# Attention projections in five token blocks of 384, 384, 384, 416 and 480 tokens instead of five blocks of 384 and one of 128

## The chip, the cores and the metric

One core of one Trainium2 chip. The metric is the device time of one execution in microseconds (us). "Before" took 1542.9 us, the median of 3 runs (1540.59 to 1543.96). Profiles come from one execution each.

## The reference, cut to what matters

The result is `x + A(xn) + B(xn)` with `xn` the normalized input of 2048 tokens by 1024. `B` is a mixer with an MLP; the change doesn't touch it. `A` is attention over 64 segments of 32 tokens with 8 memory rows that pass from one segment to the next:

```python
for s in range(n_seg):                       # 64 segments of 32 tokens
    h = jnp.concatenate([mem, xs], axis=1)   # 8 memory rows + 32 tokens
    q, k, v = (jnp.einsum('btd,dhe->bhte', h, W) for W in (Wq, Wk, Wv))   # 32 heads of 128
    p = _softmax(jnp.where(mask, q @ k.T * scale, -1e9))
    o = jnp.einsum('bhte,hed->btd', p @ v, Wo)
    mem = o[:, :M, :]
    outs.append(o[:, M:, :])
```

The kernel computes all segments in parallel. It keeps one speculated memory row for each later segment (the first has 8), so there are 2048 + 71 = 2119 columns to project. A check at the end decides whether a serial path is needed; it isn't in these runs.

## The kernel before: the parts that matter

A "tile" is three segments: 96 tokens and 3 memory rows, 99 columns (the first 106; the last, with one segment, 33). A block is four tiles: about 396 columns. The last 128 tokens form a sixth block of one full and one 33-column tile, run together with the fifth block as one group. For each block and each group of four heads (eight "head groups") the kernel projects queries and keys, computes scores, normalizes, transposes the probabilities by a DMA, and multiplies them with the values.

```python
groups = ((0,), (1,), (2,), (3,), (4, 5))
LAT = 10.0
# ... for each group, each head group hg:
for w, dsts, scale in ((wq, QTs, QSCALE), (wk, KTs, None)):
    for hh in range(4):
        for B, dst in zip(Bs, dsts):
            proj(B, w, hh, dst, scale)                       # 8 matmuls
            tick(8 * (B["nb"] / 2400 + 0.0025), ...)         # see below
        # ... output projection of the block before, in pieces, each with a tick
```

```python
def proj(B, w, hh, dst, scale):
    nb = B["nb"]
    ps = psum.tile([P, 512], F32, tag="mm", bufs=4)
    for k in range(KT):     # KT = 8; blocks 0 and 5 read one run of columns, the others four pieces of 99 (step 104)
        nc.tensor.matmul(ps[:, :nb] ..., w[:, k, hh * P:(hh + 1) * P], B["rhs"](k), start=(k == 0), stop=(k == KT - 1))
    # ... copied to dst by ScalarE
```

`tick` is a schedule made at build time. It advances an estimated clock, issues at most one pending load item (half a weight matrix, or all the values of a block), and emits at most one score item and one output item that are due. Outputs are due `LAT` = 10 us after their scores:

```python
def tick(us, blocked=None):
    clock[0] += us
    turn[0] += 1
    if turn[0] % every == 0:      # every = 1
        load_some(1)
    # ... emit one due score item ("S") and one due output item ("O")
```

The values of the 128-token block are four small transfers, which make one load item:

```python
nc.sync.dma_start(V[0:96, 0, :], V_d[r:r + 96, cs_])
nc.sync.dma_start(V[0:32, 1, :], V_d[r + 96:r + 128, cs_])
nc.sync.dma_start(V[96:99, 0, :], Vr_d[67:70, cs_])
nc.sync.dma_start(V[32:33, 1, :], Vr_d[70:71, cs_])
```

The transposes of the probabilities stand in the same SyncE queue:

```python
nc.vector.tensor_tensor(Pn[:T, :, :T], e[:T, :, :T], rs[:T, :].unsqueeze(2).to_broadcast((T, 4, T)), op=ALU.mult)
# ...
nc.sync.dma_start_transpose(PTr, Pn[:rows].rearrange("p h k -> p (h k)"))
```

## Time and profile before

| | before |
|---|---|
| time, first runs | 1542.9 us (3), with two more 1541.85 us (5) |
| span of the profiled execution | 1545.1 us |
| TensorE busy | 98% |
| fourth block, from its first projection to the fifth's | 140.2 us |
| last group (blocks 4 and 5), from its first projection to the closing matmuls of the memory rows | 211.6 us |

From the head of the page of before, with busy us, share of the span and number of instructions of each engine:

```profile
span 1545.1 us, 25390 instructions
PE 1514.8 (98%) x10308; PEld 839.7 (54%) x10382; DVE 523.8 (34%) x1092; ACT 513.9 (33%) x1218; POOL 192.5 (12%) x272
PEclk9999999999999999999999999999999999999999
```

TensorE sets the time: it is never idle for long, at full granted clock but for its two ends and one stretch of 3.4 us at half clock near 598 us, before the attention. What one matmul costs can't be read from the groups. These lines are from the groups by shape of before (busy us, mean ns of one):

```profile
L639 PE MATMUL ps<-hTb,wt 128*128 128x396 bf16 x2048 | 387.6, 332 | 0.0
L639 PEld LDWEIGHTS <-wt 128*128 128x128 bf16 x3072 | 264.5, 97 | 148.1 <-DMA wt<-in_A_Wq_dram 2.1
...
L639 PE MATMUL ps<-hTb,wt 128*128 128x132 bf16 x512 | 40.0, 221 | 0.0
```

A mean of 221 ns for 132 columns suggests that small matmuls are wasteful. They aren't: matmuls overlap. The cost is the distance from one start to the next. These lines are from TensorE's timeline of before (start us, length us; consecutive instructions merged):

```profile
1308.39 0.35 PE L678 MATMUL psO<-PT,V 99*128 99x99 bf16 x4 [1.15 <-DMA PT<-Pn]
1308.58 1.52 PE L639 MATMUL ps<-hTb,wt 128*128 128x396 bf16 x8
1309.93 0.35 PE L654 MATMUL psS<-KT,QT 128*99 128x99 bf16 x4
1310.12 0.62 PE L639 MATMUL ps<-hTb,wt 128*128 128x132 bf16 x8
1310.58 0.34 PE L678 MATMUL psO<-PT,V 99*128 99x99 bf16 x4
```

Eight matmuls of 396 columns take 1309.93 - 1308.58 = 1.35 us, 169 ns each; eight of 132 take 0.46 us, 57.5 ns each. Over all neighbours in the trace the means are 169.4 and 57.6 ns. "Start-to-start" below is this distance.

The first line also shows the one real wait of the attention: output matmuls that wait for the transposed probabilities. The line of TensorE's waits in the last group of before (us in total, times, longest):

```profile
PE psO L678 <- DMA PT<-Pn: 3.8, 5, 1.6
```

The profile counts idle time there, 3.8 us; the start-to-start excess over a plain matmul at these places is 4.6 us, because a matmul's modelled end overlaps the wait. SyncE's queue shows why in part. The longest of these waits ends at 1435.06 us. Below are the output in TensorE's timeline, SyncE's timeline ahead of it, and two lines of SyncE's waits in the last group:

```profile
1435.06 0.35 PE L678 MATMUL psO<-PT,V 99*128 99x99 bf16 x4 [1.57 <-DMA PT<-Pn]
```

```profile
1425.68 0.50 SPq L724 DMA_DIRECT2D wt<-in_A_Wk_dram  x1
1426.28 1.24 SPq L669 DMA_TRANSPOSE PT<-Pn  x1
1427.61 0.56 SPq L623 DMA_DIRECT2D V<-V_scratch  x1
1428.22 0.37 SPq L628 DMA_DIRECT2D V<-Vmem_scratch  x1
1428.75 0.32 SPq L630 DMA_DIRECT2D V<-V_scratch  x1
1429.12 0.46 SPq L631 DMA_DIRECT2D V<-V_scratch  x1
1429.63 0.59 SPq L632 DMA_DIRECT2D V<-Vmem_scratch  x1
1430.27 0.31 SPq L633 DMA_DIRECT2D V<-Vmem_scratch  x1
1432.45 7.32 SPq L669 DMA_TRANSPOSE PT<-Pn  x4
```

So the five waits of this profile have two origins. By start-to-start excess, two (0.75 and 0.45 us) follow a transpose issued 3.7 and 3.6 us late behind a weight load; two (1.7 and 0.4 us) follow one issued at most 0.9 us late that took 8.7 and 7.0 us to land; one (1.3 us) has both, 2.2 us late and 6.5 us to land.

The stretches of the third and fourth block and the last group in before (stretch, its us, then busy us of each engine, clock, DMA share, GB/s):

```profile
1011.10:1150.90 139.80, 139.59 (x961) 80.98 (x962) 64.70 (x136) 63.61 (x160) 9.99 (x16) 1.00 0.77 191
1150.90:1291.10 140.20, 139.86 (x961) 80.81 (x962) 64.53 (x138) 63.12 (x160) 11.73 (x18) 1.00 0.82 197
1291.10:1502.70 211.60, 207.20 (x1769) 129.11 (x1776) 98.62 (x225) 96.29 (x293) 8.11 (x16) 1.00 0.56 131
```

Only the last group has time in which TensorE (the first busy number) isn't busy: 4.4 us.

### The profile page before, as it was taken

The numbers are of one execution on the slowest core, as the hardware profiler recorded it, in microseconds if no ns is written. First come the engines' busy times: TensorE is split into PE (matmuls) and PEld (weight loads), VectorE is DVE, ScalarE is ACT, GpSimd is POOL, SyncE is SP. The second block draws the span as 40 slices with busy tenths as digits, with TensorE's granted clock in tenths as the row PEclk, the third lists the DMA queues.
The fourth block names the chain that finished last, engine by engine and source line by source line (L and its number), as shares of the span: only waits on it lengthen the run. The fifth ranks groups of instructions, "written<-read, shape, count | busy, mean of one in ns | idle before, by whom it ended". The sixth has DMA issues, their size and how long they took to land. (4 is left out here: it accounts for less than half of the span.)

```text
span 1545.1 us, 25390 instructions
## 1 busy us (share of the span) xinstructions
PE 1514.8 (98%) x10308; PEld 839.7 (54%) x10382; DVE 523.8 (34%) x1092; ACT 513.9 (33%) x1218; POOL 192.5 (12%) x272
## 2 busy tenths in 40 slices
PE   7999999999999999999999999999999999999998
PEld 7844444444444444444456645654665566466654
DVE  8284010000200111111246624651663365235541
ACT  5533202103012011111156614651662366056620
POOL 5232020221211241010000011002000200100001
PEclk9999999999999999999999999999999999999999
DMA  7679543452353998542389947992997599458611
GB/s 251 182 213 311 205 148 125 143 184 83 130 164 87 215 275 273 173 124 83 123 231 252 235 129 179 246 237 73 239 239 175 129 249 227 111 130 198 136 45 50
DMA packets 288601, 270.39 MB, mean 175 GB/s; under 512 B 137459, under 2 KB 255368, under 8 KB 288480
## 3 DMA queue, kind: packets, MB, share of 16 engines
q1 hardware_dynamic: 265088, 185.53, 47.0%
q0 software_dynamic: 23392, 83.19, 16.8%
q8 instruction: 83, 1.36, 0.4%
q14 instruction: 38, 0.31, 0.1%
HBM read 190.73 MB, written 46.73 MB: 154 GB/s over the span
## 5 line engine op out<-in xcount | busy, mean ns | idle before, releaser
L639 PE MATMUL ps<-hTb,wt 128*128 128x396 bf16 (+2 forms) x3072 | 514.9, 314 | 1.3 <-DMA wt<-in_A_Wq_dram 1.3
L639 PEld LDWEIGHTS <-wt 128*128 128x128 bf16 x3072 | 264.5, 97 | 148.1 <-DMA wt<-in_A_Wq_dram 2.1
L569 PE MATMUL ps<-wt,xT 128*128 128x512 bf16 x1004 | 222.0, 381 | 4.1 <-ACT Vs L571 3.1
L697 PE MATMUL pso<-wo_sb,oX 128*128 128x512 bf16 x1000 | 223.2, 379 | 1.4 <-issue 0.2
L515 PE MATMUL ps<-xn3T,w_sb 128*128 128x512 bf16 x896 | 195.9, 379 | 1.1 <-ACT h3T L516 1.1
L540 PE MATMUL ps<-w_sb,h3T 128*128 128x512 bf16 x872 | 194.3, 379 | 1.2
L569 PEld LDWEIGHTS <-xT 128*128 128x128 bf16 x1024 | 100.6, 98 | 125.3 <-issue 5.6
L516 ACT ACTIVATE h3T<-ps 128x512 bf16<-128x512 f32 x112 | 66.5, 597 | 292.0 <-PE ps L515 289.0
L697 PEld LDWEIGHTS <-oX 128*128 128x128 bf16 x1024 | 98.9, 98 | 115.3
L645 ACT CAST KT<-ps 128x396 bf16<-128x396 f32 (+1 forms) x192 | 87.1, 456 | 189.6 <-PE ps L639 186.5
L515 PEld LDWEIGHTS <-w_sb 128*128 128x128 bf16 x896 | 86.8, 98 | 103.9 <-issue 1.3
L540 PEld LDWEIGHTS <-h3T 128*128 128x128 bf16 x896 | 86.8, 98 | 102.8
L660 DVE TENSOR_REDUCE sums<-sm 99x4 f32<-99x396 f32 (+1 forms) x176 | 97.6, 555 | 113.9 <-ACT sm L658 113.9
L647 ACT ACTIVATE QT<-ps 128x396 bf16<-128x396 f32 (+1 forms) x192 | 89.4, 469 | 108.0 <-PE ps L639 79.8
L656 DVE TENSOR_TENSOR sm<-psS,c_mask_reg_sb 99x396 f32<-99x396 f32 x160 | 91.4, 572 | 90.1 <-PE psS L654 89.9
L571 ACT CAST Vs<-ps 128x512 bf16<-128x512 f32 x64 | 37.2, 586 | 238.4 <-PE ps L569 152.6
L658 ACT ACTIVATE sm<-sm 99x396 f32<-99x396 f32 (+1 forms) x176 | 92.7, 527 | 65.9 <-DVE sm L656 64.7
L573 DVE CAST Vs<-ps 128x512 bf16<-128x512 f32 x64 | 44.2, 692 | 181.8 <-PE ps L569 156.8
L666 DVE TENSOR_TENSOR Pn<-sm,rs 99x396 bf16<-99x396 f32 (+1 forms) x176 | 99.0, 562 | 10.2 <-DMA PT<-Pn 4.0
L541 DVE TENSOR_TENSOR R<-ps,R 128x512 f32<-128x512 f32 x32 | 22.1, 692 | 231.4 <-PE ps L540 215.0
L704 POOL DMA_DIRECT2D out_dram<-ot x32 | 17.5, 546 | 575.8 <-DVE ot L703 569.9
L679 ACT CAST oX<-psO 128x384 bf16<-128x384 f32 x176 | 82.5, 469 | 16.8 <-PE psO L678 16.7
(116 smaller groups left out, 979.5 us busy)
## 6 DMA issues: line engine op xcount, KB each, us to landing
wt<-in_A_Wq_dram SPq DMA_DIRECT2D x78, 512.0 KB
wt<-in_A_Wk_dram SPq DMA_DIRECT2D x78, 512.0 KB
wt<-in_A_Wv_dram POOLq DMA_DIRECT2D x24, 1024.0 KB, 7.1
V_scratch<-Vs SPq DMA_DIRECT2D x32, 512.0 KB
V<-V_scratch SPq DMA_DIRECT2D x40, 384.0 KB
w_sb<-in_B_w_dram SPq DMA_DIRECT2D x9, 1024.0 KB
R_scratch<-x POOLq DMA_DIRECT2D x16, 512.0 KB, 4.4
R<-R_scratch SPq DMA_DIRECT2D x16, 512.0 KB
```

The costliest lines, as they stand in the source:

```text
L515: nc.tensor.matmul(ps[:].rearrange("p (n t) -> p n t", t=P), w3_sb[:, k, f * P:(f + 1) * P], xn3T[tb][:, :, k, :], start=(k == 0), stop=(k ...
L540: nc.tensor.matmul(ps[:], h3T[:, f, j * P:(j + 1) * P], w4_sb[:, f, ch * 512:(ch + 1) * 512], start=(f == 0), stop=(f == FT - 1))
L569: nc.tensor.matmul(ps[:], xT[:, m4 * 4 + j, k, :], wv[:, k, :], start=(k == 0), stop=(k == KT - 1))
L639: nc.tensor.matmul(ps[:, :nb] if B["b"] in (0, 5) else ps[:, :nb].rearrange("p (t c) -> p t c", t=4), w[:, k, hh * P:(hh + 1) * P], B["rhs ...
L645: nc.scalar.copy(o, i)
L647: nc.scalar.mul(o, i, scale)
L656: nc.vector.tensor_tensor(sm[:T, :, :T], S3, t["mask"][:].unsqueeze(1).to_broadcast((T, 4, T)), op=ALU.add)
L658: nc.scalar.activation(e[:T, :, :T], sm[:T, :, :T], ACTF.Exp, scale=LN2)
L660: nc.vector.tensor_reduce(ss, e[:T, :, :T], axis=AX.X, op=ALU.add)
L666: nc.vector.tensor_tensor(Pn[:T, :, :T], e[:T, :, :T], rs[:T, :].unsqueeze(2).to_broadcast((T, 4, T)), op=ALU.mult)
L679: nc.scalar.copy(oX[:, hs_, t["tok"]:t["tok"] + nt], O3[:, :, 0:nt])
L697: nc.tensor.matmul(self.ps[:], self.oX[:, h, self.gl * P:(self.gl + 1) * P], wo_sb[:, h, self.cc], start=(h == 0), stop=(h == H - 1))
```

## The change

The intent: no extra 128-token block. Its 33-column tile joins the fourth block (4 x 99 + 33 = 429 columns) and its full tile the fifth (5 x 99 = 495 columns, within the 512 of the tile `ps` that a projection writes). The 512 matmuls of 132 columns, their weight loads and 64 evacuations (ScalarE's copies of the results) go. The core of the diff; address arithmetic, buffers and names are cut:

```diff
-        if b == 5:
-            segs = (3, 1)
-        else:
-            segs = (3, 3, 3, 3)
+        gis = list(range(4 * b, 4 * b + 4)) + ([21] if b == 3 else [20] if b == 4 else [])
@@ block_setup
+            elif b == 3:
+                hTb = early.tile([P, KT, 432], BF16, tag="hTb")
+                for t in tl:
+                    nc.gpsimd.dma_start(hTb[:, :, t["c0"]:t["c0"] + t["ntok"]], xT_d[...])
+                    d = t["c0"] + t["ntok"]
+                    nc.vector.tensor_copy(hTb[:, :, d:d + t["nm"]], MZ[:, :, t["r0"]:t["r0"] + t["nm"]])
             else:
-                hTb = early.tile([P, KT, 4, 104], BF16, tag="hTb")
+                hTb = early.tile([P, KT, nt, 104], BF16, tag="hTb")     # nt = 5 in the last block
@@ load_values: the four loads of block 5 go; block 3 has two small loads more
+            if b == 3:
+                nc.sync.dma_start(V[0:32, 4, :], V_d[S - 32:S, cs_])
+                nc.sync.dma_start(V[32:33, 4, :], Vr_d[70:71, cs_])
@@
-        groups = ((0,), (1,), (2,), (3,), (4, 5))
+        groups = ((0,), (1,), (2,), (3,), (4,))
```

The attention output of the 33-column tile is kept in the last 32 columns of block 3's output buffer, which block 4 goes on to use. The small sums `xsum` move from the constants to a buffer that is freed earlier.

More of the change, by code (lines that the diff above doesn't have):

```diff
@@ L141 @@
     nc.vector.memset(neghalf[:], -0.5)
-    xsum = cpool.tile([P, KT, NSEG], BF16)
     sums = cpool.tile([P, NTILE * 8, 4], F32)
@@ L158, in tiles_of @@
     def tiles_of(b):
-        if b == 5:
-            segs = (3, 1)
-        else:
-            segs = (3, 3, 3, 3)
-        out_, c, t0 = [], 0, 4 * b
-        for i, s in enumerate(segs):
+        gis = list(range(4 * b, 4 * b + 4)) + ([21] if b == 3 else [20] if b == 4 else [])
+        out_, c = [], 0
+        for i, gi in enumerate(gis):
+            s = 1 if gi == 21 else 3
             first = b == 0 and i == 0
@@ L167, in tiles_of @@
             msk = mask_first if first else (mask_reg if s == 3 else mask_last)
-            r0 = 0 if first else 7 + 3 * (t0 + i)
-            out_.append(dict(c0=c, ntok=s * SEG, nm=nm, T=s * SEG + nm, mask=msk, r0=r0, tok=i * 96, i=i, gi=t0 + i))
+            r0 = 0 if first else 7 + 3 * gi
+            out_.append(dict(c0=c, ntok=s * SEG, nm=nm, T=s * SEG + nm, mask=msk, r0=r0, tok=i * 96, i=i, gi=gi))
             c += s * SEG + nm
@@ L195 @@
             w3ctx = bctx.enter_context(ExitStack())
+            xctx = bctx.enter_context(ExitStack())
+            xsum = xctx.enter_context(tc.tile_pool(name="xs", bufs=1)).tile([P, KT, NSEG], BF16)
             w3_pool = w3ctx.enter_context(tc.tile_pool(name="w3", bufs=1, side="right"))
@@ L549 @@
                         nc.gpsimd.dma_start(R_v[:, n, :], R1[:])
+            xctx.close()
             vsp = vctx.enter_context(tc.tile_pool(name="vsp", bufs=3, side="right"))
@@ L600, in block_setup @@
                 hTb, rhs = hTb0, lambda k: hTb0[:, k, :nb]
-            elif b == 5:
-                hTb = early.tile([P, KT, 136], BF16, tag="hT5", bufs=1)
-                nc.gpsimd.dma_start(hTb[:, :, 0:96], xT_d[:, :, a:a + 96])
-                nc.gpsimd.dma_start(hTb[:, :, 99:131], xT_d[:, :, a + 96:a + 128])
-                nc.vector.tensor_copy(hTb[:, :, 96:99], MZ[:, :, 67:70])
-                nc.vector.tensor_copy(hTb[:, :, 131:132], MZ[:, :, 70:71])
+            elif b == 3:
+                hTb = early.tile([P, KT, 432], BF16, tag="hTb")
+                for t in tl:
+                    nc.gpsimd.dma_start(hTb[:, :, t["c0"]:t["c0"] + t["ntok"]], xT_d[:, :, 96 * t["gi"]:96 * t["gi"] + t["ntok"]])
+                    d = t["c0"] + t["ntok"]
+                    nc.vector.tensor_copy(hTb[:, :, d:d + t["nm"]], MZ[:, :, t["r0"]:t["r0"] + t["nm"]])
                 rhs = lambda k: hTb[:, k, :nb]
             else:
-                hTb = early.tile([P, KT, 4, 104], BF16, tag="hTb")
+                nt = len(tl)
+                hTb = early.tile([P, KT, nt, 104], BF16, tag="hTb")
                 r0 = tl[0]["r0"]
-                for i in range(4):
+                for i in range(nt):
                     nc.gpsimd.dma_start(hTb[:, :, i, 0:96], xT_d[:, :, a + 96 * i:a + 96 * (i + 1)])
-                nc.vector.tensor_copy(hTb[:, :, :, 96:99], MZ[:, :, r0:r0 + 12].rearrange("p k (t r) -> p k t r", t=4))
+                nc.vector.tensor_copy(hTb[:, :, :, 96:99], MZ[:, :, r0:r0 + 3 * nt].rearrange("p k (t r) -> p k t r", t=nt))
                 rhs = lambda k: hTb[:, k, :, 0:99]
@@ L616, in block_setup @@
                     t["c0"] = 104 * i
-            return dict(b=b, tiles=tl, nb=nb, ntok=ntok, rhs=rhs, cols=nb if b in (0, 5) else 416)
+            return dict(b=b, tiles=tl, nb=nb, ntok=ntok, rhs=rhs, cols=nb if b in (0, 3) else 104 * len(tl))
         def load_values(B, V, hg):
             b, cs_ = B["b"], slice(hg * 512, (hg + 1) * 512)
-            r = 384 * b
-            if b < 5:
-                nc.sync.dma_start(V[0:96, 0:4, :], V_d[r:r + 384, cs_].rearrange("(t p) c -> p t c", p=96))
-                if b == 0:
-                    nc.sync.dma_start(V[96:106, 0, :], Vr_d[0:10, cs_])
-                    nc.sync.dma_start(V[96:99, 1:4, :], Vr_d[10:19, cs_].rearrange("(t j) c -> j t c", j=3))
-                else:
-                    nc.sync.dma_start(V[96:99, 0:4, :], Vr_d[7 + 12 * b:19 + 12 * b, cs_].rearrange("(t j) c -> j t c", j=3))
-            else:
-                nc.sync.dma_start(V[0:96, 0, :], V_d[r:r + 96, cs_])
-                nc.sync.dma_start(V[0:32, 1, :], V_d[r + 96:r + 128, cs_])
-                nc.sync.dma_start(V[96:99, 0, :], Vr_d[67:70, cs_])
-                nc.sync.dma_start(V[32:33, 1, :], Vr_d[70:71, cs_])
+            r, n = 384 * b, 5 if b == 4 else 4
@@ new lines, in load_values @@
+            nc.sync.dma_start(V[0:96, 0:n, :], V_d[r:r + 96 * n, cs_].rearrange("(t p) c -> p t c", p=96))
+            if b == 0:
+                nc.sync.dma_start(V[96:106, 0, :], Vr_d[0:10, cs_])
+                nc.sync.dma_start(V[96:99, 1:4, :], Vr_d[10:19, cs_].rearrange("(t j) c -> j t c", j=3))
+            else:
+                nc.sync.dma_start(V[96:99, 0:n, :], Vr_d[7 + 12 * b:7 + 12 * b + 3 * n, cs_].rearrange("(t j) c -> j t c", j=3))
+            if b == 3:
+                nc.sync.dma_start(V[0:32, 4, :], V_d[S - 32:S, cs_])
+                nc.sync.dma_start(V[32:33, 4, :], Vr_d[70:71, cs_])
@@ L635, in proj @@
         def proj(B, w, hh, dst, scale):
-            nb = B["nb"]
+            nb, nt = B["nb"], len(B["tiles"])
+            flat = B["b"] in (0, 3)
             ps = psum.tile([P, 512], F32, tag="mm", bufs=4)
             for k in range(KT):
-                nc.tensor.matmul(ps[:, :nb] if B["b"] in (0, 5) else ps[:, :nb].rearrange("p (t c) -> p t c", t=4), w[:, k, hh * P:(hh + 1) * P], B["rhs"](k), start=(k == 0), stop=(k == KT - 1))
-            if B["b"] in (0, 5):
+                nc.tensor.matmul(ps[:, :nb] if flat else ps[:, :nb].rearrange("p (t c) -> p t c", t=nt), w[:, k, hh * P:(hh + 1) * P], B["rhs"](k), start=(k == 0), stop=(k == KT - 1))
@@ L641, in proj @@
+            if flat:
                 o, i = dst[:, hh, :nb], ps[:, :nb]
             else:
-                o, i = dst[:, hh, :].rearrange("p (t c) -> p t c", t=4)[:, :, 0:99], ps[:, :nb].rearrange("p (t c) -> p t c", t=4)
+                o, i = dst[:, hh, :].rearrange("p (t c) -> p t c", t=nt)[:, :, 0:99], ps[:, :nb].rearrange("p (t c) -> p t c", t=nt)
             if scale is None:
@@ L670, in scores, with outputs @@
             return PTr
-        def outputs(t, hg, PTr, V, oX):
+        def outputs(t, hg, PTr, V, oX, at):
             T, nt = t["T"], t["ntok"]
@@ L678, in outputs @@
                 nc.tensor.matmul(O3[:, hh, :], V[:T, t["i"], hh * P:(hh + 1) * P], PTr[:T, hh, :T], start=True, stop=True)
-            nc.scalar.copy(oX[:, hs_, t["tok"]:t["tok"] + nt], O3[:, :, 0:nt])
+            nc.scalar.copy(oX[:, hs_, at:at + nt], O3[:, :, 0:nt])
             nq = t["nm"]
@@ L720, in stage_loads @@
             wq, wk = ready or (wtile(), wtile())
-            Vs = [qkv.tile([P, len(B["tiles"]), 512], BF16, tag=f"V{B['b'] // 5}", bufs=3, name=f"V{B['b']}") for B in Bs]
+            Vs = [qkv.tile([P, len(B["tiles"]), 512], BF16, tag="V", bufs=3, name=f"V{B['b']}") for B in Bs]
             for w, src in () if ready else ((wq, Wq_v), (wk, Wk_v)):
@@ L757 @@
                 wq, wk, Vs = ahead
-                QTs = [qkv.tile([P, 4, B["cols"]], BF16, tag=f"QT{B['b'] // 5}", name=f"QT{B['b']}") for B in Bs]
-                KTs = [qkv.tile([P, 4, B["cols"]], BF16, tag=f"KT{B['b'] // 5}", name=f"KT{B['b']}") for B in Bs]
+                QTs = [qkv.tile([P, 4, B["cols"]], BF16, tag="QT", name=f"QT{B['b']}") for B in Bs]
+                KTs = [qkv.tile([P, 4, B["cols"]], BF16, tag="KT", name=f"KT{B['b']}") for B in Bs]
                 if hg == 2 and gi_ + 1 < len(groups):
@@ L782, with s_item @@
                     if B["b"] not in oXs:
-                        if B["b"] == 5:
-                            oXs[5] = early.tile([P, H, B["ntok"]], BF16, tag="hTb", name="oX5")
-                        else:
-                            oXs[B["b"]] = abig.tile([P, H, B["ntok"]], BF16, tag="oX", name=f"oX{B['b']}")
-                    def s_item(t=t, hg=hg, QT=QT, KTt=KTt, V=V, oX=oXs[B["b"]], due=due, gi_=gi_):
+                        oXs[B["b"]] = oX_last if B["b"] == 4 else abig.tile([P, H, 512 if B["b"] == 3 else 384], BF16, tag="oX", name=f"oX{B['b']}")
+                        oX_last = oXs[B["b"]]
+                    oX, at = oXs[B["b"]], 480 if t["gi"] == 21 else t["tok"]
+                    def s_item(t=t, hg=hg, QT=QT, KTt=KTt, V=V, oX=oX, at=at, due=due, gi_=gi_):
                         PTr = scores(t, hg, QT, KTt)
                         def o_item():
-                            outputs(t, hg, PTr, V, oX)
+                            outputs(t, hg, PTr, V, oX, at)
                             return 0.18
@@ L796 @@
                     smalls.append((due, ("S", gi_), s_item))
-            outs = [Out(oXs[B["b"]], 3 * B["b"] + gl, gl, ch) for B in Bs for gl in range(B["ntok"] // P) for ch in range(2)]
+            outs = [Out(oXs[B["b"]], 3 * B["b"] + gl, gl, ch) for B in Bs for gl in range(4 if B["b"] == 4 else 3) for ch in range(2)]
         head, rest = outs[:4], outs[4:]
```

## The prediction

> **What bounds it.** TensorE: the page gives 1514.8 busy of 1545.1 us (98%) at full granted clock. A group's mean duration is no cost here, because matmuls overlap; I take start-to-start distances from the timeline: 512 columns 215.7 ns, 403 columns 171, 396 columns in four pieces of 99 169.4, 132 columns 57.6. The Trainium skill ("TensorE: Matmul & The Clock Gate", section "Wait — 56ns, not 53.3ns?") states N / 2.4 GHz + about 2.5 ns warm; the flat shapes agree (132: 55.0 + 2.6; 512: 213.3 + 2.4), the shape in four pieces pays 4.4. Weight loads (97 ns in the groups) are hidden even behind 57.6 ns matmuls, so a small block is not a wasteful matmul.
>
> **What the change removes, adds and moves.** The last group's projections drop from 512 matmuls of 396 plus 512 of 132 columns to 512 of 495 (five pieces); the fourth block's 512 go from 396 to 429 (flat). Columns are the same (2119 per weight tile); 512 matmuls and weight loads go. Score, output and closing matmuls keep their counts (22 tiles of 8 head groups); the 33-row tile moves to the fourth block. ScalarE loses 64 evacuations (about 0.28 us each, 18 us), but at 33% busy that is off the path. Estimate: before 169.4 + 169.4 + 57.6 = 396.4 ns per set, after about 181.4 + 210.6 = 392; 512 times 4.4 ns is 2.3 us, all on the path.
>
> **Waits.** In the last group (about 1310 to 1490 us) the output matmuls wait for the transposed probabilities (the DMA PT<-Pn): start-to-start excesses of 1.7, 1.3, 0.75, 0.45 and 0.4 us, 4.6 us in all, while the middle blocks lose about 0.3 each. From scores to output the schedule gives about 10.4 us; the median transposition lands in 7, but in the last group the time from probabilities to the transpose's issue on SyncE's queue rises to 2.0 us (upper quartile) against under 0.1 in the middle blocks: that queue also carries six loads of values per head group there (four small ones for the 128-token block) besides four of weights and six transposes. After, the last block has two value loads and five transposes, the fourth four and five. I expect the last block to lose under 1 us, the fourth 1 to 1.5: some 2 us saved net, less certain than the matmul term.
>
> The output projection, the tail and the first 1160 us: unchanged.
>
> **Predicted: 1538.6 us** (1542.9 - 2.3 - 2.0), range 1535 to 1542.5. Faster by over 2%: 1%; within 2%: 98.5%; slower by over 2%: 0.5%.
>
> **What would show it.** Right: 512 matmuls each of 429 and 495 columns, start-to-start 181-182 and 209-212 ns; ScalarE about 15 us less busy; the fourth block's window grows by about 10 us, the last's falls by about 14; PT waits of the last block below 1 us, of the fourth 1 to 1.5. Wrong: 495 columns costing over 215 ns; PT<-Pn waits of 4 us or more still there, moved to the fourth block; a new wait for ScalarE or for V loads, since five tiles now meet eight projections.
>
> **What would make it wrong.** The wait term: transposes come in the fourth block as densely as in the old last group (13 queue entries per about 13.4 us against 16 per 16.6), so the gain may be 2.3 us alone (about 1540.6), or the waits may grow. The runs of before differ among themselves by 3.4 us, more than half of what I predict.

## More of the kernel before

```profile
SPq L669 <- DMA wt<-in_A_Wk_dram: 11.2, 6, 2.9
...
SPq L633 <- DMA wt<-in_A_Wk_dram: 2.1, 2, 1.1
```

The transpose that this output waited for is the one at 1426.28, between a weight load and six value loads. It was issued 0.44 us after its probabilities were done and landed at 1435.02, 8.7 us after its issue (median of the last group's tiles: 2.7): it was late on its way, not in the queue. The next transpose, at 1432.45, was late in the queue: it was issued 3.1 us after its probabilities, and landed in time for its output all the same. The trace shows what held it. SyncE's DMAs signal their landing on eight semaphores in turn, and before each issue SyncE waits for the semaphore that it will use. The eighth entry before this transpose is the weight load at 1425.68; that load landed at 1432.39, and the transpose was issued 0.06 us later. The line of 11.2 us counts six such waits, one in each of six head groups.

## The result, and the profile after

After took 1540.13 us, the median of 5 runs (1538.93 to 1540.65), against 1541.85 us of before (5 runs). The ratio is 0.9981, with a 95% interval of 0.9966 to 0.9996. Ratios here are the mean time of one kernel's runs over that of the other's runs of the same rounds, so they are not quite the ratio of the medians. In a later batch after took 1540.01 us against 1544.77 us: 0.9966 (0.9953 to 0.9979). So the gain is 3 to 5 us: 2.9 us by the first ratio (interval 0.6 to 5.2) and 5.2 us by the second (3.2 to 7.3). Both are far within 2%.

From the head of the page of after:

```profile
span 1538.9 us, 24379 instructions
PE 1516.0 (99%) x9870; PEld 810.3 (53%) x9870; DVE 522.2 (34%) x1094; ACT 506.1 (33%) x1154; POOL 192.5 (13%) x272
```

The busy us of TensorE are no measure of the gain. They rose by 1.2 us while the span fell by 6.2 us, and its instruction count fell by 438 where the program has 512 matmuls less, so 74 more records were missing from the trace of before. The new shapes among the groups of after:

```profile
L638 PEld LDWEIGHTS <-wt 128*128 128x128 bf16 x2560 | 233.9, 97 | 168.3 <-DMA wt<-in_A_Wq_dram 1.8 <-issue 0.7
L638 PE MATMUL ps<-hTb,wt 128*128 128x396 bf16 x1024 | 193.6, 332 | 0.0
L638 PE MATMUL ps<-hTb,wt 128*128 128x495 bf16 x512 | 117.3, 373 | 0.0
L638 PE MATMUL ps<-hTb,wt 128*128 128x429 bf16 x512 | 102.7, 345 | 0.0
```

TensorE's timeline of after, once in the fourth and once in the last block:

```profile
1270.96 1.62 PE L638 MATMUL ps<-hTb,wt 128*128 128x429 bf16 x8
1272.41 0.34 PE L677 MATMUL psO<-PT,V 99*128 99x99 bf16 x4
...
1401.15 1.85 PE L638 MATMUL ps<-hTb,wt 128*128 128x495 bf16 x8
1402.84 0.35 PE L653 MATMUL psS<-KT,QT 128*99 128x99 bf16 x4
```

Start-to-start: 1.45 us for 8, 181 ns; 1.69 us for 8, 211 ns. The means over the trace are 181.9 and 211.1 ns.

The same three stretches in after:

```profile
1011.00:1151.60 140.60, 140.01 (x965) 81.09 (x963) 64.54 (x140) 62.81 (x161) 10.87 (x17) 1.00 0.74 190
1151.60:1301.80 150.20, 150.20 (x1016) 82.11 (x1014) 70.72 (x162) 68.64 (x181) 10.86 (x17) 1.00 0.73 187
1301.80:1496.40 194.60, 194.60 (x1211) 98.55 (x1210) 91.06 (x198) 83.84 (x209) 8.07 (x16) 1.00 0.54 138
```

In the fourth and last blocks TensorE is busy all the time; the list of its waits there is empty. In the third block, whose program did not change except that it prepares the next block's input, a wait of TensorE has come in, and on VectorE its origin:

```profile
PE psS L653 <- ACT KT L644: 0.6, 1, 0.6
```

```profile
1081.09 0.19 DVE L606 COPY hTb<-MZ 128x24 bf16<-128x24 bf16 x1 [1.37 <-DMA hTb<-xT_scratch]
...
1084.88 0.18 DVE L606 COPY hTb<-MZ 128x24 bf16<-128x24 bf16 x1 [2.32 <-DMA hTb<-xT_scratch]
1084.97 0.56 DVE L655 TENSOR_TENSOR sm<-psS,c_mask_reg_sb 99x396 f32<-99x396 f32 x1
```

In the new layout of the fourth block's input the copies of memory rows lie between the loaded columns, and each waits for the load written before it. The next tile's scores start on VectorE right after the last copy, at 1084.97, having stood behind its wait of 2.3 us; the delay then passes to ScalarE and to TensorE (a_mz_first below tests this).

The lengths of the stretches, by the start of the first projection matmul of each block and of the closing memory matmuls, are the sharpest measure, since they hold no launch or start-up:

| us | third block | fourth | last | fourth + last |
|---|---|---|---|---|
| before, first profile | 139.8 | 140.2 | 211.6 | 351.7 |
| before, second profile | 139.8 | 139.8 | 210.0 | 349.8 |
| after, first | 140.5 | 150.2 | 194.6 | 344.8 |
| after, second | 140.4 | 150.2 | 194.6 | 344.8 |

After gives the same length twice; before does not.

### The profile page after: what moved, and what is told of

The parts are those of the page before. It is cut to its first block, busy times and chain, and to the rows that moved or that the text cites. A ratio compares the mean times of both kernels' runs of the same rounds, so it can differ in the third digit from the quotient of the medians. Undisturbed runs are those within 1.5% of the kernel's fastest.

```text
span 1538.9 us, 24379 instructions
## 1 busy us (share of the span) xinstructions
PE 1516.0 (99%) x9870; PEld 810.3 (53%) x9870; DVE 522.2 (34%) x1094; ACT 506.1 (33%) x1154; POOL 192.5 (13%) x272
## 5 line engine op out<-in xcount | busy, mean ns | idle before, releaser
L638 PE MATMUL ps<-hTb,wt 128*128 128x396 bf16 (+3 forms) x2560 | 509.9, 343 | 1.0 <-DMA wt<-in_A_Wq_dram 1.0
L638 PEld LDWEIGHTS <-wt 128*128 128x128 bf16 x2560 | 233.9, 97 | 168.3 <-DMA wt<-in_A_Wq_dram 1.8
L644 ACT CAST KT<-ps 128x396 bf16<-128x396 f32 (+3 forms) x160 | 82.0, 513 | 221.8 <-PE ps L638 219.9
L659 DVE TENSOR_REDUCE sums<-sm 99x4 f32<-99x396 f32 (+2 forms) x176 | 97.5, 554 | 113.2 <-ACT sm L657 113.2
L657 ACT ACTIVATE sm<-sm 99x396 f32<-99x396 f32 (+2 forms) x176 | 92.7, 527 | 76.3 <-DVE sm L655 75.7
L646 ACT ACTIVATE QT<-ps 128x396 bf16<-128x396 f32 (+3 forms) x160 | 83.8, 525 | 74.9 <-PE ps L638 50.2
L665 DVE TENSOR_TENSOR Pn<-sm,rs 99x396 bf16<-99x396 f32 (+2 forms) x176 | 98.9, 562 | 6.2 <-DMA PT<-Pn 0.2
L678 ACT CAST oX<-psO 128x384 bf16<-128x384 f32 (+1 forms) x176 | 82.5, 469 | 9.0 <-PE psO L677 8.5
```

The source lines that it names most:

```text
L638: nc.tensor.matmul(ps[:, :nb] if flat else ps[:, :nb].rearrange("p (t c) -> p t c", t=nt), w[:, k, hh * P:(hh + 1) * P], B["rhs"](k), star ...
L644: nc.scalar.copy(o, i)
L646: nc.scalar.mul(o, i, scale)
L657: nc.scalar.activation(e[:T, :, :T], sm[:T, :, :T], ACTF.Exp, scale=LN2)
L659: nc.vector.tensor_reduce(ss, e[:T, :, :T], axis=AX.X, op=ALU.add)
L678: nc.scalar.copy(oX[:, hs_, at:at + nt], O3[:, :, 0:nt])
```

## The experiments

Theory M: TensorE pays for columns plus a small fixed amount for each matmul, and weight loads are hidden. Theory Q: the waits of the last group come of the many entries of SyncE's queue, or of their coming in a burst; from its experiments came theory B (the burst alone). Rival S: they come of too short a distance from scores to outputs. Rival W: small matmuls are bounded by their weight loads. Three times below are worked out from the trace's records, as medians or quartiles over the tiles of a block: "issue delay" is the time from the end of the probabilities' last operation to the start of the transpose on SyncE's queue, "to landing" is from the last score matmul to the transpose's last semaphore update, and "waits" are start-to-start excesses of over 0.2 us at output matmuls that wait for it.

| run | fourth + last, us | ratio to before | 95% |
|---|---|---|---|
| c_before_again | 349.8 | 0.9992 | 0.9978 to 1.0005 |
| b_v5_pool | 352.6 | 1.0016 | 0.9999 to 1.0033 |
| b_later_out | 347.5 | 0.9977 | 0.9960 to 0.9995 |
| b_paced | 346.6 | 0.9988 | 0.9974 to 1.0003 |
| a_burst | 352.0 | 1.0020 | 1.0006 to 1.0034 |
| a_split | 346.2 | 0.9982 | 0.9968 to 0.9996 |
| a_mz_first | 344.8 | 0.9976 | 0.9962 to 0.9990 |
| a_flat | 344.0 | 0.9950 | 0.9935 to 0.9966 |
| after_again | 344.8 | 0.9966 | 0.9953 to 0.9979 |
| a_halves | 347.5 | 1.0001 | 0.9987 to 1.0014 |
| a_flat_late | 344.0 | 0.9951 | 0.9927 to 0.9974 |

The first four shared a chip, so did the next four, and the last three. The medians of before were 1544.57, 1543.42 and 1544.77 us there. A ratio's interval is about 2 us wide to each side, so the stretches tell more than the ratios where the question is 1 us.

### c_before_again: before against itself

No edit.

> The kernel before, unchanged, timed against itself. It tells the noise of a ratio and whether the first profile of before (span 1545.1 us, 4.6 us of start-to-start excess at output matmuls of the last group that wait for PT<-Pn) is a typical execution. Theory Q (the waits are a fixed property of the program): ratio 1.000 within 0.15%, and the new profile shows again 3.5 to 5.5 us of such excess. Rival R (the first profile caught an unlucky execution): the new profile shows under 2.5 us of excess and a span of 1540 to 1543 us.

Measured: 1543.23 us, ratio 0.9992; span of the profiled execution 1540.2 us. TensorE's waits in the last group:

```profile
PE psO L678 <- DMA PT<-Pn: 2.4, 2, 1.6
```

The start-to-start excess was 2.9 us, between what the two theories expected. The wait is a property of the program, but its size varies from execution to execution, and the first profile of before (span 1545.1 us) had caught a larger one. So the 6.2 us between the two profiled spans overstate the gain.

### b_v5_pool: the small value loads moved to another queue

```diff
-                nc.sync.dma_start(V[0:96, 0, :], V_d[r:r + 96, cs_])
+                nc.gpsimd.dma_start(V[0:96, 0, :], V_d[r:r + 96, cs_])
# and so for the other three
```

> Before, with the four small value loads of the 128-token block issued from GpSimd instead of SyncE; nothing else. Theory Q (the transposes are issued late because they stand behind these loads in SyncE's queue): time from probabilities to issue of the transposes in the last group falls from 2.0 us (upper quartile) to under 0.5, the PT waits of the last group from 4.6 us to under 1.5, and the time by 1 to 4 us. Rival S (the wait comes of the short distance from scores to outputs, 10.3 us in this group, with a transpose that simply takes long): issue delay may fall, but waits stay over 3 us and the time stays within 0.5 us.

Measured: 1548.06 us, ratio 1.0016. The issue delay vanished (upper quartile 0.08 us, from 2.0), exactly as theory Q expected, and the waits did not, as rival S expected:

```profile
PE psO L678 <- DMA PT<-Pn: 4.0, 6, 1.0
```

The transposes were issued earlier and took longer: from issue to landing 6.7 us at the upper quartile, against 4.0 in before. To landing stayed at 9.7 us (before: 9.8). So standing behind these four loads in the queue is not what makes the transposes late; take the queue away, and they are late elsewhere. The Trainium skill ("DMA: Bandwidth & Descriptors", section "Issuing engines are not separate DMA queues") says that DMAs issued from different engines run on the same 16 DMA engines, and that issuing from several saves only the issue time; this run fits that: the issue delay went, the landing stayed at 9.7 us. It isn't a pure test: the profile counts loads issued by GpSimd under another queue (q0, software_dynamic, instead of q1, hardware_dynamic), and the end of this kernel was also about 2 us longer, for a reason not followed up.

### b_later_out: outputs later after their scores

```diff
-                        smalls.append((clock[0] + LAT, ("O", gi_), o_item))
+                        smalls.append((clock[0] + (12.0 if gi_ == 4 else LAT), ("O", gi_), o_item))
```

> Before, with the outputs of the last group scheduled 12 instead of 10 us after their scores (12.4 instead of 10.3 us of TensorE work between them); the DMA queue is untouched. Theory Q: transposes are still issued late (upper quartile about 2 us), but the later outputs hide most of it: waits under 1.5 us. Rival S: waits under 0.5 us as well, with no need of a late issue. Both expect the time 1 to 4 us down; it bounds what the wait term is worth in the clock without touching any matmul of the projections.

Measured: 1542.01 us, ratio 0.9977. The issue delay stayed (upper quartile 1.9 us), the waits inside the group were gone; one of 1.0 us remained at its start, where an output of the block before stands. Fourth and last together took 347.5 us. The waits are worth 2 to 4 us, and by this run alone both late transposes and early outputs can be blamed: they are the two ends of one slack.

### b_paced: the same loads, spread

```diff
-        def tick(us, blocked=None):
+        def tick(us, blocked=None, load=True):
-            if turn[0] % every == 0:
+            if load and turn[0] % every == 0:
...
-  tick(8 * (B["nb"] / 2400 + 0.0025), blocked=...)
+  tick(8 * (B["nb"] / 2400 + 0.0025), blocked=..., load=B["b"] != 5)
```

> Before, with the loads of the last group issued only after projections of the 384-token block, so that the same 16 entries per head group are spread over the group instead of standing in a burst. Theory Q in the form 'it is the count of entries that matters': issue delay and waits within a third of before's (2.0 us, 4.6 us). Theory Q in the form 'it is the burst': issue delay under 0.7 us, waits under 2 us. Rival S: waits stay over 3 us.

Measured: 1542.06 us, ratio 0.9988. Issue delay 0.37 us at the upper quartile, to landing 7.9 us instead of 9.8, no wait of output matmuls for transposes in the last group. The last group's stretch, in which TensorE was idle for 4.4 us in before:

```profile
1288.00:1494.90 206.90, 206.32 (x1770) 129.29 (x1776) 98.58 (x225) 95.46 (x293) 8.11 (x16) 1.00 0.56 133
```

Same entries, same bytes, and a distance from scores to outputs that did not grow (median from the end of a tile's scores to its output 10.2 us, 10.5 in before): the burst, and neither the count nor the distance alone, was the cause. Of the transposes issued over 1 us late, one was held by a weight load eight entries back here, six in before. Fourth and last took 346.6 us, so the burst costs before 3.1 us (second profile) to 5.1 us (first). The clock's ratio, 0.9988 with before alone at 0.9992 in the same batch, can't show that by itself.

In before a load item goes out with each projection, and every second projection is the 132-column one, which takes 0.46 us. In after all projections are long: this paces the loads by the way. After also gives more time from scores to outputs, which the prediction didn't count: 11.4 us (median) in the fourth block and 11.1 in the last, against 10.4 and 10.5 in before. It isn't needed for the result: the longest time to landing in these blocks is 8.7 us (8.9 in the second profile), against 12.2 in the last group of before.

### a_burst: the burst put back into after

```diff
-                load_some(1)
+                load_some(per_tick[0])          # 2 in the fourth and last blocks, else 1
```

> After, with two load items instead of one after each projection in the fourth and last blocks, so that the weights and values of the next head group (2 MB and 0.4 MB) are asked for within about 3.4 us instead of 7 us; same transfers, same matmuls. Theory B (the transposes land late where the loads stand in a burst, be it in SyncE's queue or in the DMA engines): PT waits come back, 1 to 4 us in these two blocks (after: 0), and scores to landing rises at the upper quartile from 7.6 and 6.9 us to over 9. Rival C (it is the count of queue entries, which is not changed): no waits, landing within 0.5 us of after's, time within 0.7 us of after's (1540.1).

Measured: 1547.6 us, ratio 1.0020: slower than before. In the fourth block the issue delay rose to 3.2 us and the time to landing to 10.7 us (upper quartiles; after: 0.4 and 7.6). TensorE's waits in the fourth and last blocks, where after has none:

```profile
PE psO L677 <- DMA PT<-Pn: 4.8, 4, 1.9
```

All of these fall on outputs of the fourth block, which has 13 queue entries for each head group; in the last, with 11, landing rose from 6.9 to 8.3 us, still under the 11 us until the outputs. Theory B holds: the four transposes waited for stand behind other entries of the queue for 3.2 to 5.1 us and then take 3.9 to 6.3 us to land. One edit of the load schedule loses more than the whole change gains: 352.0 against 344.8 us. Not all of it is waiting, though. 5.4 us are start-to-start excess at these four outputs; 1.6 us more follow the longest wait, where the granted clock fell to half for 3.4 us. Two lines of TensorE's timeline, and the stretch with its clock (0.54):

```profile
1309.43 0.34 PE L677 MATMUL psO<-PT,V 99*128 99x99 bf16 x4 [1.93 <-DMA PT<-Pn]
1309.88 3.43 PE L638 MATMUL ps<-hTb,wt 128*128 128x495 bf16 x8
...
1309.50:1313.20 3.70, 3.70 (x18) 1.60 (x18) 2.08 (x5) 1.10 (x3) 0.00 (x0) 0.54 0.34 67
```

These eight matmuls follow each other at 413 ns instead of 211. After the wait of 1.57 us in before the clock stayed full.

### a_split: the matmuls put back, the schedule kept

```diff
+            if B["b"] == 4:
+                for i0, i1 in ((0, 4), (4, 5)):
+                    for k in range(KT):
+                        nc.tensor.matmul(ps[:, 99 * i0:99 * i1]..., w[:, k, ...], B["rhs"](k)[:, i0:i1], start=(k == 0), stop=(k == KT - 1))
```

> After, with each 495-column matmul of the last block done as one of 396 and one of 99 columns, with the same loads and the same schedule: the matmul term alone, put back (512 more matmuls and weight loads). Theory M (a matmul costs columns / 2.4 GHz plus a fixed 2.5 ns, about 0.4 ns for each piece, and weight loads stay hidden): the pair takes about 169.4 + 44 = 213.4 ns against 211.1, 1.2 us in all, and the last block's window grows by that. Rival W (a 99-column matmul does not hide its weight load of 97 ns): the pair takes 240 ns or more, over 15 us in all.

Measured: 1541.22 us, ratio 0.9982. The 99-column matmuls follow at 44.0 ns, the 396-column ones at 169.4: 213.5 ns for the pair, as theory M expected. The last block grew by 1.35 us, from 194.6 to 196.0, and no waits came back. That is 2.6 ns for each added matmul. Rival W falls: even 44 ns hide a weight load whose record lasts 97.

### a_mz_first: the copies ahead of the loads

```diff
                 for t in tl:
-                    nc.gpsimd.dma_start(hTb[...], xT_d[...])
                     d = t["c0"] + t["ntok"]
                     nc.vector.tensor_copy(hTb[:, :, d:d + t["nm"]], MZ[...])
+                for t in tl:
+                    nc.gpsimd.dma_start(hTb[...], xT_d[...])
```

> After, with the five small copies of memory rows into the fourth block's input put ahead of its loads from memory, so that VectorE does not stand waiting for these loads. Theory D (that wait, 3.7 us on VectorE with one of 0.8 us on TensorE behind it, is a new cost of the change's layout): the wait hTb<-xT_scratch on VectorE and the TensorE wait for ScalarE's KT are gone, and the time falls by 0.3 to 0.8 us. Rival: the wait moves to another engine, and the time stays within 0.2 us.

Measured: 1540.11 us, ratio 0.9976. VectorE's wait for these loads is gone and so is TensorE's for ScalarE; the third block takes 139.9 us instead of 140.5 and 140.4. Theory D holds: 0.5 to 0.6 us of new cost came with the layout. The clock can't resolve it.

### a_flat: all blocks without gaps

```diff
-            elif b == 3:
-                hTb = early.tile([P, KT, 432], BF16, tag="hTb")
+            else:
+                hTb = early.tile([P, KT, 496], BF16, tag="hTb")
# the branch with step 104 is dropped; copies ahead of the loads as in a_mz_first
```

> After, with the inputs of blocks 1, 2 and 4 laid out without gaps as that of block 3 is, so that a matmul reads one run of columns instead of four or five pieces of 99 (small copies ahead of the loads, as in a_mz_first). Theory P (each piece costs about one 2.4 GHz cycle): 396 columns fall from 169.4 to about 167.7 ns, 495 from 211.1 to about 209, together 1024 x 1.7 + 512 x 2.1 = 2.8 us less, plus what a_mz_first gives. Rival: the start-to-start distances stay, or the odd offsets of 99 columns make the score matmuls' weight loads slower, and nothing is gained.

Measured: 1537.55 us against 1543.42 us, ratio 0.9950. It beats before, and each of its six runs is below all five of a_mz_first on the same chip (0.9976). After itself was not timed beside it: it had 0.9981 and 0.9966 in its two batches. Start-to-start falls to 167.6 ns for 396 and 209.3 ns for 495 columns. That is 1.8 ns less in both, with four pieces and with five, so on these two shapes it is a fixed cost of the gapped operand and not one cycle for each piece, as theory P had it. 1536 x 1.8 ns is 2.8 us. The score matmuls did not get slower (46.7 ns).

### after_again: after once more

No edit.

> After, unchanged, on the same chip and with the same runs of before as the two next kernels. Theory: ratio to before 0.997 to 0.9985 as at first (0.9981), no PT wait over 0.5 us in the fourth and last blocks, one wait of about 0.7 us of TensorE for ScalarE's KT near 1090 us. If the small waits of after were luck, PT waits of 2 us or more show up in these blocks.

Measured: 1540.01 us, ratio 0.9966. No wait in the fourth and last blocks, the wait near 1091 us is there again (0.4 us; 0.6 in the first profile). One wait of 0.8 us in the first block, as in the first profile of before; the second profile of before has none.

### a_halves: five times the matmuls that the change removed

```diff
-            for k in range(KT):
-                nc.tensor.matmul(ps[:, :nb] ..., B["rhs"](k), ...)
+            for c0, c1 in ((0, nb // 2), (nb // 2, nb)):
+                for k in range(KT):
+                    nc.tensor.matmul(ps[:, c0:c1], w[:, k, ...], B["rhs"](k)[:, c0:c1], start=(k == 0), stop=(k == KT - 1))
```

> The flat layout with every projection matmul cut into two halves of 198 to 248 columns: 2560 more matmuls and weight loads, five times what the change took away, with the columns unchanged. Theory M (a fixed 2.5 ns for each matmul, weight loads hidden): start-to-start 85.0 ns for 198 columns and 105.8 for 248, 6.4 us longer than the flat kernel of the last batch (ratio to before about 0.995 + 0.0042 = 0.999). Rival W (weight loads of 97 ns bound a stream of small matmuls): 198 columns take 97 ns or more, at least 12 ns x 4096 = 49 us longer.

Measured: 1544.81 us, ratio 1.0001. The span is 6.6 us longer than a_flat's (1542.5 against 1535.9), but that is no measure: a_flat's profile has 6.8 us at half clock near 600 us, before the attention, and this one none. Two lines of TensorE's timeline:

```profile
1099.94 1.53 PE L630 MATMUL ps<-hTb,wt 128*128 128x198 bf16 x16
1101.31 0.34 PE L645 MATMUL psS<-KT,QT 128*99 128x99 bf16 x4
```

Sixteen matmuls of 198 columns in 1.37 us are 85.6 ns each (85.4 over the trace, expected 85.0). The stretches of the second to the last block, which hold 2048 of the added matmuls, are together 6.6 us longer than a_flat's: 3.2 ns for each, more than the 2.5 expected. The halves of 248 columns, which start at an odd column, follow at 107.4 ns instead of the 105.8 expected. So theory M holds at five times the dose in its form, with a fixed cost that differs with the shape; rival W, which asked for 49 us, is out.

### a_flat_late: flat, and outputs 11 us after scores

```diff
-        LAT = 10.0
+        LAT = 11.0
```

> The flat layout with outputs scheduled 11 instead of 10 us after their scores in all blocks. The flat kernel still had 1.3 us of PT waits of TensorE in its first blocks; theory B expects these to fall under 0.5 us and the ratio to before to 0.994 to 0.9955 (flat: 0.995). If more outputs in flight get in each other's way (buffers of transposed probabilities, five), the time grows by 0.5 us or more instead.

Measured: median 1536.16 us, ratio 0.9951 (a_flat: 0.9950), with one run of 1546.28 us that widens the interval. The transposes' waits fell to 0.4 us of idle time, as expected, but the stretch of fourth and last did not shorten (344.0 us in both). Nothing that the clock shows is gained over a_flat.

## Why the prediction was right, point by point

It held: 1540.13 us lie within 1535 to 1542.5, and the forecast gain of 4.3 us lies between the 2.9 and 5.2 us of the two batches.

- "TensorE bounds, columns decide, small blocks are not wasteful": shown by a_split and a_halves. The Trainium skill ("TensorE: Matmul & The Clock Gate", section "Wait — 56ns, not 53.3ns?") gives N / 2.4 GHz and about 2.5 ns for a warm matmul; each added matmul cost 2.6 ns in a_split and 3.2 ns in a_halves.
- "512 times 4.4 ns is 2.3 us": 396.4 ns became 181.9 + 211.1 = 393.0 ns; 512 x 3.4 ns is 1.7 us. Compared without waits, b_paced (346.6) and after (344.8 us) differ by 1.8 us. The term was about 0.5 us too large, because each new shape cost 0.5 ns more than estimated.
- "Some 2 us saved net" of waits: mis-sized. The waits of the two blocks went to zero, in both profiles of after. What they had cost was 3.1 us in one profile of before and 5.1 us in the other. Against this stands 0.6 us of a new wait in the third block. The 4.6 us of the first profile were taken as the fixed size of the wait; they were one draw.
- The step that failed is the reason given for it: "that queue also carries six loads of values per head group there (four small ones for the 128-token block) besides four of weights and six transposes". The count of entries alone is not the cause. The fourth block of after has as dense a queue and no waits, where the prediction had 1 to 1.5 us; b_paced keeps the count and loses the waits; b_v5_pool takes the four small entries out of the queue and keeps the waits; and in before itself the longest wait was for a transpose issued 0.44 us after its probabilities. What the runs show in its place is the rate at which loads are asked for, set here by the 0.46 us projections of the small block.
- "The fourth block's window grows by about 10 us, the last's falls by about 14": +10.0 and -16.9 in the first profiles; +10.4 and -15.3 in the second ones.
- "ScalarE about 15 us less busy": 513.9 to 506.1, 7.8 us. The wider evacuations (495 columns: 586 and 572 ns against 504 and 492) took back part of it. It was off the path, as said.
- "a new wait for ScalarE": one came, of 0.6 us, but not because five tiles meet eight projections: it started at the copies on VectorE that wait for loads, and a_mz_first removed it.

The sum for a usual execution, from the second profiles: 1.8 us of matmuls and 3.1 us of waits, less 0.6 us of the new wait, is 4.3 us. That this equals the forecast is partly luck: one term was too large, the other too small. What stays open is the second of the two ways in which a burst holds transposes back. The late issue is seen in the traces of before (SyncE waits for a weight load eight entries back) and of a_burst (entries stand in line). The late landing, 7.0 and 8.7 us in before and up to 9.3 us in b_v5_pool for transposes issued in time, is seen too, but no run tells what the transfers wait for on the DMA engines.

## What to carry to other kernels

Cost a merge of small matmuls by start-to-start distances and not by mean durations: where weight loads are hidden, as here, a matmul merged away saves about 3 ns (2.6 to 3.4 in these runs), and no more. When a build-time schedule issues loads by the number of compute steps, a change of the steps' length changes the pacing of the loads, and transfers with a deadline, here the transposes, can land late for it; the pacing can be set by itself. Before taking a wait of one profile for the size of a gain, take a second profile of the same kernel, and look at the granted clock of both.

## What the Trainium skill lacked or had wrong

- "TensorE: Matmul & The Clock Gate", section "Back-to-back issue gap", gives for a stream of weight load and matmul pairs a sustained ~81 ns at 128 columns and ~131 ns at 512. Here such pairs run at 44.0 ns (99 columns), 57.6 (132), 85.4 (198) and 215.8 (512). The page's formula N / 2.4 + 2.5, which it says under-counts at small N in such streams, fits these four within 0.4 ns; 248 columns from an odd offset, at 107.4 ns, are 1.6 ns over it.
- The same page, Part 3 ("What overlaps and what doesn't"), says that weight loads overlap with matmuls in flight only when they use other row groups, though an earlier sentence of that part also names a background weight buffer. Here loads of 128 rows by 128 columns (97 ns by their records) are hidden behind matmuls of all 128 rows that follow at 44.0 ns.
- No page that was read has a cost of an operand with gaps. A moving operand in four or five pieces of 99 columns costs 1.8 ns for each matmul over one contiguous run (169.4 against 167.6 ns, 211.1 against 209.3).
- No page that was read has the cost of changing to a smaller array shape; the point belongs to "TensorEngine Tiling (Array Packing)", which has a drain on a change of tiling mode but no figure for it. In after a 429-column matmul is followed at 275 ns instead of 182 by one with 33 weight columns, and at 278 ns by one with 33 rows; on the way back the next matmul follows at 104 to 110 ns, where one of the same small shape follows at 25. Between shapes of 99 and 128 nothing of the kind shows. No run tells what causes it.
- No page that was read has the eight completion semaphores on which SyncE's DMAs take turns here: in before a transpose was issued 0.06 us after the landing of the weight load eight entries earlier, 3.1 us after its data were ready. Whether the program or the chip sets that number, no run tells.
